# A retention and low-rank mixer kernel on one core: the first two batches handled by pairs of heads

## The chip, the core and the metric

The kernel runs on one core of one Trainium2 chip. The core has a matrix engine (TensorE, PE in the profile, with its weight loads shown apart as PEld), three elementwise engines (VectorE = DVE, ScalarE = ACT, GpSimd = POOL) and a queue engine (SyncE = SP) that here issues loads. Each engine runs its own list of instructions in order; engines wait for one another through semaphores. Matrix products are written to PSUM, a small memory of eight banks, from which DVE or ACT must copy them out. The metric is the time of one execution on the device, in microseconds (us).

## The reference

Eight batches, eight heads, 576 positions, head size 64. First a decayed causal attention without softmax, then a token mixing of rank 32 and a channel MLP with a residual:

```
scores = scale * q @ k.T ;  gamma_h = 1 - 2**(-5-h)
Dmat   = gamma_h ** (i - j)  where i >= j, else 0
x      = (scores * Dmat) @ v            # heads side by side: (B, 576, 512)
u      = x + ((x.T @ U) @ V).T          # U: 576 x 32, V: 32 x 576
out    = u + relu(u @ w_ch1) @ w_ch2    # w_ch1: 512 x 2048, w_ch2: 2048 x 512
```

Inputs and output are float32; the kernel multiplies in bfloat16.

## The kernel before

The eight batches are four couples. A couple's 1152 tokens are cut into nine chunks of 128; chunk 4 (`J`) holds the last 64 tokens of the first batch and the first 64 of the second. The decay is split into a factor on each row of `v` (`vscale`) and one on each output row (`qscale`). With that, a chunk needs four matrix steps: transposes of q and k (T), scores (SC) that DVE multiplies with a triangle of ones (mask), the product with `v` (RV), and the product of q with the running state (QS), which is itself a sum of k-transposed times v (ST). DVE then scales the result into `x` (XS). The mixer makes `a` from U and x (MA), adds V times `a` to x (MH, giving `u`) and needs `u` transposed (`uT`). Then `y1` (w1 times `uT`, 16 blocks f, line 477, Relu on ACT at line 482) and `y2` (line 511, output at line 500 and its store from POOL's queue at line 503).

From the third batch on, transposes are done by DMA, and `merge` lays attention and mixer of the next batch between the matrix products of the present one. The first two batches have their own code, and only this is touched by the change:

- `startup` (line 779) does batch 0 up to `uT`. q, k and v come in units of 256 tokens and all eight heads (`load_u`): two neighbouring tokens lie on one partition, so a DMA piece is 2 x 64 floats, 512 bytes. Batch 0 has units 0 and 1, batch 1 units 2 and 3; the 64 tokens in J are loaded apart (pieces of 256 bytes). POOL casts q and k (line 592) and scales v (line 596). T_u (607), SC_u (635), RV_u (661), QS_u (670), ST_u (687) are PE's steps of a unit. Scores and RV use halves of the array, 64 rows each. `warm(n)` (189) gives PE n products that nobody reads.
- At the end of `startup`, `x` is transposed on PE into four PSUM tiles `xT` (859), V times `a` is added there (874), and four copies (882, 884) give `uT` of batch 0.
- `first_stretch` (line 886) lays batch 1's units, its mixer (394, 421) and its transposes of `u` (`MT`, 448) between the 16 `y1` blocks of batch 0 (`y(n)` emits n of them), starts `y1` of batch 1 and returns what is left of it to `merge`.
- SP's queue carries every load of q, k, v in program order through 15 buffers `stage`. POOL's queue carries w1 (four blocks, line 195), w2 (201), and stores, between its own casts.
- PSUM: `ps_sc` (one buffer of two banks: scores), `ps_o` (one of two banks: RV and QS), `ps_s` (one bank) and `ps_big` (three).

The order of instructions on each engine is the order of the code: the schedule is written by hand.

Of the kernel before, what the change touches and what calls it, by code (L numbers as in the profile page):

```python
# [35 lines left out]
def kernel(  # L36
# [18 lines left out]
    HALF = 64  # L55
    NHP = H // 2
# [3 lines left out]
    J = 4  # L60
# [32 lines left out]
    triU = consts.tile([P, 2, P], BF16, name="triU")  # L93
    iotaU = consts.tile([P, 2, P], FP32, name="iotaU")
    posU = consts.tile([P, 4, 2, H], FP32, name="posU")
    vscaleU = consts.tile([P, 4, 2, H], FP32, name="vscaleU")
# [17 lines left out]
    def early_consts():  # L114
# [3 lines left out]
            posU, pattern=[[2 * P, 4], [1, 2], [0, H]], base=0, channel_multiplier=2,  # L118
# [3 lines left out]
            iotaU, pattern=[[-1, 2], [1, P]], base=0, channel_multiplier=-2,  # L122
# [7 lines left out]
        for h in range(H):  # L130
            nc.vector.memset(lngt[:, :, h], lng[h])
        nc.vector.tensor_scalar_add(posU[:, 2:4], posU[:, 2:4], -float(4 * P - HALF))
        nc.vector.tensor_tensor(
            out=posU.rearrange("p u j h -> p (u j) h"),
            in0=lngt[:, 0:8, :], in1=posU.rearrange("p u j h -> p (u j) h"), op=ALU.mult)
        nc.scalar.activation(out=vscaleU, in_=posU, func=AF.Exp, bias=lnb, scale=-1.0)
        nc.vector.tensor_scalar(
            out=triU[0:HALF], in0=iotaU[0:HALF], scalar1=0.0, scalar2=None, op0=ALU.is_ge)
        nc.vector.tensor_scalar(
            out=triU[HALF:P], in0=iotaU[HALF:P], scalar1=-float(P), scalar2=None,  # L140
            op0=ALU.is_ge)
# [24 lines left out]
    def make_u():  # L166
        nc.scalar.activation(out=U_E[:, 0:J, :], in_=U_f[:, 0:J, :], func=AF.Copy)
        nc.scalar.activation(out=U_E[0:HALF, J, :], in_=U_f[0:HALF, J, :], func=AF.Copy)

        ps = ps_s.tile([P, 5, R], FP32, tag="pss", name="pu_o")  # L170
        nc.tensor.matmul(ps, swap, U_E, start=True, stop=True)
        nc.scalar.activation(out=U_O[0:HALF, 1:5, :], in_=ps[0:HALF, 0:4, :], func=AF.Copy)
        nc.scalar.activation(out=U_O[HALF:P, :, :], in_=ps[HALF:P, :, :], func=AF.Copy)
# [59 lines left out]
    def cast_qk(pr, i, rows=slice(0, P), eng=None):  # L233
# [4 lines left out]
        if eng is not None:  # L238
            for j in (1, 0):
                eng.tensor_copy(  # L240
                    out=t[rows, j, :], in_=c["f", j][rows].rearrange("p h d -> p (h d)"))
            return
# [222 lines left out]
    def y1_items(par, by_seg=False):  # L465
        nch = 4 + par
        segs = [(0, 4)] if par == 0 else [(0, 3), (3, 2)]
        items = []

        def Y1(f, seg):  # L470
            if f == 0 and seg == 0:
                st["y1", par] = y1_pool.tile(
                    [P, NF, nch * P], BF16, tag=f"y1{par}", name="y1")
# [86 lines left out]
    un = [dict() for _ in range(4)]  # L560
    st["x", 0] = x_pool.tile([P, NI, dm], BF16, tag="x", name="xt")

    def unit_i0(u):
        return 2 * u + (1 if u >= 2 else 0)

    def load_u(u, which):
        b = u // 2
        t0 = 2 * P * (u % 2) + HALF * b
        for j in which:
            dram = (q, k, v)[j]  # L570
            for hh in range(2):
                t = stage.tile([P, H, D], FP32, tag="stage", name="stage_t")
                un[u]["f", j, hh] = t
                nc.sync.dma_start(  # L574
                    out=t.rearrange("p (h j) d -> p h (j d)", j=2),
                    in_=dram[b, 4 * hh:4 * hh + 4, t0:t0 + 2 * P, :].rearrange(
                        "h (p j) d -> p h (j d)", j=2),
                )

    def unit_views(u, j, hh):  # L580
        if j not in un[u]:
            un[u][j] = qk_pool.tile([P, 2, dm], BF16, tag="qk", name="qk")
        w = slice(hh * 4 * D, (hh + 1) * 4 * D)
        return (un[u][j][:, :, w].rearrange("p j (h d) -> p h j d", d=D),
                un[u]["f", j, hh].rearrange("p (h j) d -> p h j d", j=2))

    def cast_u(u, j, hh, eng):
        o, f = unit_views(u, j, hh)
        if eng is nc.scalar:
            nc.scalar.activation(out=o, in_=f, func=AF.Copy)  # L590
        else:
            eng.tensor_copy(out=o, in_=f)  # L592

    def scale_u(u, hh, eng):
        o, f = unit_views(u, 2, hh)
        eng.tensor_tensor(
            out=o, in0=f,
            in1=vscaleU[:, u, :, 4 * hh:4 * hh + 4].rearrange("p j h -> p h j")[
                :, :, :, None].to_broadcast([P, 4, 2, D]),
            op=ALU.mult,  # L600
        )

    def T_u(u, j, eng):
        pst = ps_big.tile([P, 2 * NHP, P], BF16, tag="big", name="pst")
        for jj in range(2):
            for hp in range(NHP):
                nc.tensor.transpose(
                    pst[:, jj * NHP + hp, :], un[u][j][:, jj, hp * P:(hp + 1) * P], ident)
        t = qkT_pool.tile([P, 2 * NHP, P], BF16, tag="qkT", name="qkT")
        un[u]["T", j] = t  # L610
        o, i_ = t, pst
        if j == 0:

            o = t.rearrange("p a b -> p (a b)").rearrange(
                "p (hp t j) -> p j hp t", hp=NHP, j=2)
            i_ = pst.rearrange("p (j hp) t -> p j hp t", j=2)
        if eng is nc.scalar:
            nc.scalar.activation(out=o, in_=i_, func=AF.Copy)
        else:
            eng.tensor_copy(out=o, in_=i_)  # L620

    def qT(u):
        return un[u]["T", 0].rearrange("p a b -> p (a b)").rearrange(
            "p (hp t) -> p hp t", hp=NHP)

    def SC_u(u, hh, pool_, tag):
        psc = pool_.tile([P, 2, NHP, P], FP32, tag=tag, name="psc")
        kT, qt = un[u]["T", 1], qT(u)
        for hp in range(2):
            for jj in range(2):  # L630
                for s in range(2):
                    for hl in range(2):
                        r = slice(hl * HALF, (hl + 1) * HALF)
                        m = slice(s * HALF, (s + 1) * HALF)
                        nc.tensor.matmul(  # L635
                            psc[m, hl, hp * 2 + jj, :], kT[r, jj * NHP + 2 * hh + hp, m],
                            qt[r, 2 * hh + hp, s * P:(s + 1) * P], start=True, stop=True,
                        )
        un[u]["psc", hh] = psc

    def mask_u(u, hh):
        ret = ret_pool.tile([P, H, P], BF16, tag="ret", name="ret")
        nc.vector.tensor_tensor(  # L643
            out=ret.rearrange("p (a j) i -> p a (j i)", j=2),
            in0=un[u]["psc", hh].rearrange("p a b i -> p (a b i)").rearrange(
                "p (a ji) -> p a ji", a=4),
            in1=triU.rearrange("p j i -> p (j i)")[:, None, :].to_broadcast([P, 4, 2 * P]),
            op=ALU.mult,
        )
        un[u]["ret", hh] = ret  # L650

    def RV_u(u, hh):
        if "po" not in un[u]:
            un[u]["po"] = ps_o.tile([P, 2, dm], FP32, tag="po", name="po")
        for hp in range(2):
            for hl in range(2):
                h = 4 * hh + 2 * hp + hl
                for jj in range(2):
                    for s in range(2):
                        r = slice(s * HALF, (s + 1) * HALF)  # L660
                        nc.tensor.matmul(  # L661
                            un[u]["po"][:, s, h * D:(h + 1) * D],
                            un[u]["ret", hh][r, hl * 4 + hp * 2 + jj, :],
                            un[u][2][r, jj, h * D:(h + 1) * D],
                            start=(h == 0 and jj == 0), stop=True, skip_group_check=True,
                        )

    def QS_u(u, s, slot):
        for hp in range(NHP):
            nc.tensor.matmul(  # L670
                un[u]["po"][:, s, hp * P:(hp + 1) * P],
                qT(u)[:, hp, s * P:(s + 1) * P], sblk[:, slot, hp, :],
# [3 lines left out]
    def XS_u(u, c0=0, c1=2):  # L676
        i0, n = unit_i0(u) + c0, c1 - c0
        nc.vector.tensor_tensor(  # L678
            out=st["x", 0][:, i0:i0 + n, :].rearrange("p s (h d) -> p s h d", d=D),
            in0=un[u]["po"][:, c0:c1, :].rearrange("p s (h d) -> p s h d", d=D),  # L680
            in1=qscale[:, i0:i0 + n, :, None].to_broadcast([P, n, H, D]), op=ALU.mult,
        )

    def ST_u(u, rows, acc, start):
        for hp in range(NHP):
            for jj in range(2):
                nc.tensor.matmul(  # L687
                    acc[:, hp, :], un[u][1][rows, jj, hp * P:(hp + 1) * P],
                    un[u][2][rows, jj, hp * P:(hp + 1) * P],
                    start=(start and hp == 0 and jj == 0), stop=True,  # L690
                    skip_group_check=True,
                )

    def Sblk(acc, slot):
        for hl in range(2):
            r = slice(hl * HALF, (hl + 1) * HALF)
            nc.scalar.activation(
                out=sblk[r, slot, :, hl * D:(hl + 1) * D],
# [315 lines left out]
```

## Time and profile before

| what | value |
|---|---|
| time, median of 3 runs (lowest to highest) | 335.87 us (335.54 to 336.67) |
| span of the profiled execution, first to last instruction | 335.6 us |
| instructions | 6997 |
| PE busy | 320.9 us, 96% of the span |
| PEld, DVE, ACT, POOL busy | 179.9, 138.0, 139.2, 78.2 us |
| moved by DMA | 53.17 MB, mean 158 GB/s |
| PE, first product of `y1` (line 477) starts | 32.07 us |

PE's busy time is no measure of how full it is: products overlap, and each shows a latency of about 0.2 us. The timeline gives for a row of n products the time from the first start to the last end; the start of the next row minus the start of this one, divided by n, is what one of them really takes of PE.

### The profile page before, as it was taken

To read this page: it belongs to the slowest core of one execution; us is meant where nothing else is said; L and a number is where in the kernel's file an instruction comes from. 1 tells how busy PE (TensorE), PEld (TensorE's weight loads), DVE (VectorE), ACT (ScalarE), POOL (GpSimd) and SP (SyncE) were. 2 spreads that over 40 slices of the span, in tenths; PEclk is the share of its full clock that TensorE was granted. 3 is DMA by queue.
4 is the path that set the end of the run, shared out by engine and by line. 5 is a ranking of instruction groups with operands and counts; after the bars stand their busy time and mean duration, and the time that the engine had idled before them with its cause. 6 is when DMAs were issued, how large, how long until landed. Compare 5 with 4: busy or idle time off the path is not lost.

```text
span 335.6 us, 6997 instructions
## 1 busy us (share of the span) xinstructions
PE 320.9 (96%) x2926; PEld 179.9 (54%) x2948; DVE 138.0 (41%) x190; ACT 139.2 (41%) x290; POOL 78.2 (23%) x112
## 2 busy tenths in 40 slices
PE   6688999899999999999999999999999999999996
PEld 3375554576544445446764455457754455457644
DVE  5453346433564234534356244524365144510022
ACT  2543665776210077107850176017740264037400
POOL 5686741211231140114102220222111100110000
PEclk9955999999999999999999999999999999999999
DMA  7999999999999929994998959995933400340012
GB/s 212 239 228 266 237 217 182 187 179 223 213 249 234 234 73 192 207 198 105 198 177 190 213 123 168 195 241 71 200 76 99 142 2 1 79 126 2 0 64 94
DMA packets 151311, 53.17 MB, mean 158 GB/s; under 512 B 131984, under 2 KB 148752, under 8 KB 151280
## 3 DMA queue, kind: packets, MB, share of 16 engines
q1 hardware_dynamic: 144512, 40.40, 64.7%
q0 software_dynamic: 6768, 12.32, 14.6%
q8 instruction: 23, 0.38, 0.5%
q14 instruction: 8, 0.07, 0.1%
HBM read 36.85 MB, written 9.44 MB: 138 GB/s over the span
## 4 chain that ended last, share of the span: by engine, by line
PE 91%; SPq 2%; issue 2%; DVE 2%; DMA 1%; ACT 1%; POOL 0%
PE ps_y L477 38%; PE ps_y L511 36%; PE psc L275 3%; PE po L314 2%; PE pss L687 2%; PE pss L340 2%; DMA stage_t<-in_q_dram 1%; SPq L574 1%; PE ph L421 1%; PE ps_y L522 1%; PE pa L394 1%; PE po L300 1%; PE po L661 1%; PE xT L859 1%; DVE xt L678 1%
## 5 line engine op out<-in xcount | busy, mean ns | idle before, releaser
L477 PE MATMUL ps_y<-uT,w_sb 128*128 128x256 bf16 (+2 forms) x768 | 137.0, 328 | 1.5 <-ACT uT L452 1.4
L482 ACT ACTIVATE y<-ps_y 128x384 bf16<-128x384 f32 (+2 forms) x192 | 90.0, 489 | 114.9 <-PE ps_y L477 114.2
L511 PE MATMUL ps_y<-w_sb,y 128*128 128x512 bf16 x538 | 124.3, 379 | 1.6 <-issue 0.8
L477 PEld LDWEIGHTS <-w_sb 128*128 128x128 bf16 x768 | 71.6, 98 | 46.7 <-issue 3.1
L511 PEld LDWEIGHTS <-y 128*128 128x128 bf16 x560 | 52.4, 98 | 60.3
L500 DVE TENSOR_TENSOR o_sb<-ps_y,u 128x512 f32<-128x512 f32 (+2 forms) x38 | 25.2, 663 | 76.6 <-PE ps_y L511 74.4
L503 POOL DMA_DIRECT2D out_dram<-o_sb x31 | 17.3, 558 | 158.6 <-DVE o_sb L500 152.8
L285 DVE TENSOR_TENSOR ret<-psc,tri 128x1024 bf16<-128x1024 f32 x24 | 29.4, 1225 | 47.3 <-PE psc L275 47.3
L254 POOL TENSOR_TENSOR vt<-stage_t,vscale 128x512 bf16<-128x512 f32 (+1 forms) x29 | 30.0, 1047 | 50.6 <-DMA stage_t<-in_v_dram 50.1
L325 DVE TENSOR_TENSOR xt<-po,qscale 128x512 bf16<-128x512 f32 x27 | 18.6, 691 | 25.9 <-PE po L314 25.9
L427 DVE TENSOR_TENSOR u<-ph,xt 128x768 bf16<-128x768 f32 (+2 forms) x24 | 21.8, 951 | 13.5 <-PE ph L421 13.5
L348 ACT ACTIVATE s_sb<-pss 128x512 bf16<-128x512 f32 x24 | 14.3, 597 | 8.3 <-PE pss L340 7.3
L245 ACT ACTIVATE qk<-stage_t 128x512 bf16<-128x512 f32 x27 | 16.5, 622 | 2.1 <-DVE o_sb L500 2.1
L243 DVE CAST qk<-stage_t 128x512 bf16<-128x512 f32 x27 | 16.3, 604 | 0.0
L400 ACT ACTIVATE a_sb<-pa 128x128 bf16<-128x128 f32 x8 | 2.2, 276 | 33.0 <-PE pa L394 33.0
L643 DVE TENSOR_TENSOR ret<-psc,triU 128x1024 bf16<-128x1024 f32 x8 | 9.7, 1222 | 11.3 <-PE psc L635 11.3
L314 PEld LDWEIGHTS <-ret 128*128 128x128 bf16 x216 | 10.0, 98 | 4.2
L592 POOL CAST qk<-stage_t 128x512 bf16<-128x512 f32 x16 | 9.6, 611 | 7.0 <-DMA stage_t<-in_q_dram 5.3
L275 PEld LDWEIGHTS <-qkT 64*128 64x128 bf16 x216 | 6.1, 94 | 9.1 <-issue 8.7
L275 PE MATMUL psc<-qkT 64*128 64x128 bf16 x216 | 10.7, 219 | 0.0
L314 PE MATMUL po<-vt,ret 128*128 128x64 bf16 x216 | 10.7, 193 | 0.0
L340 PE MATMUL pss<-vt,qk 128*128 128x128 bf16 (+1 forms) x96 | 9.3, 219 | 0.0
(103 smaller groups left out, 165.5 us busy)
## 6 DMA issues: line engine op xcount, KB each, us to landing
stage_t<-in_k_dram SPq DMA_DIRECT2D x32, 256.0 KB, 4.1
stage_t<-in_q_dram SPq DMA_DIRECT2D x32, 256.0 KB, 4.9
stage_t<-in_v_dram SPq DMA_DIRECT2D x32, 256.0 KB, 5.5
out_dram<-o_sb POOLq DMA_DIRECT2D x31, 256.0 KB, 3.8
w_sb<-in_moe_w_ch_dram POOLq DMA_DIRECT2D x4, 512.0 KB, 8.4
w_sb<-in_moe_w_ch_dram POOLq DMA_DIRECT2D x8, 256.0 KB, 10.2
stage_t<-in_k_dram SPq DMA_DIRECT2D x8, 128.0 KB, 4.2
stage_t<-in_q_dram SPq DMA_DIRECT2D x8, 128.0 KB, 4.0
```

What stands on the lines that cost most here:

```text
L245: nc.scalar.activation(out=t[rows, 0, :], in_=c["f", 0][rows].rearrange("p h d -> p (h d)"), func=AF.Copy)
L254: (eng or nc.gpsimd).tensor_tensor(out=c["v"][rows], in0=c["f", 2][rows], in1=vscale[rows, i, :, None].to_broadcast([n, H, D]), op=ALU.mult,)
L275: nc.tensor.matmul(psc[:, hl, hp, :], qkT[r, NHP + hp, :], qkT[r, hp, :], start=True, stop=True,)
L285: nc.vector.tensor_tensor(out=ret.rearrange("p (hp hl) i -> p hl hp i", hl=2), in0=c["psc"], in1=m[:, None, None, :].to_broadcast([P, 2, N ...
L314: nc.tensor.matmul(c["po"][:, hl, hp * D:(hp + 1) * D], c["ret"][:, h, :], c["v"][:, h, :], start=(first and hp == 0), stop=True, skip_gro ...
L325: nc.vector.tensor_tensor(out=xt[:, i, :].rearrange("p (hp hl d) -> p hl hp d", hl=2, d=D), in0=c["po"][:, :, 0:NHP * D].rearrange("p hl ( ...
L427: nc.vector.tensor_tensor(out=st["u", par][:, i0 - base:i0 - base + n, w].rearrange("p s (c d) -> p c s d", c=2), in0=ph[k][:, :, 0:n, :], ...
L477: nc.tensor.matmul(ps[:, 0:n, :], w1_sb[:, cc, f * P:(f + 1) * P], st["uT", par][:, c0:c0 + n, cc, :], start=(cc == 0), stop=(cc == NCC - 1),)
L482: nc.scalar.activation(out=st["y1", par][:, f, c0 * P:(c0 + n) * P], in_=ps[:, 0:n, :].rearrange("p s t -> p (s t)"), func=AF.Relu)
L500: nc.vector.tensor_tensor(out=o_sb[:, 0:n], in0=ps[:, 0:n], in1=st["u", par][:, c, w], op=ALU.add)
L503: (nc.sync if last else nc.gpsimd).dma_start(out=out_flat[r0:r0 + P, w], in_=o_sb[:, 0:n])
L511: nc.tensor.matmul(ps, st["y1", par][:, f, c * P:(c + 1) * P], w2_sb[:, f, :], start=(f == 0), stop=(f == NF - 1),)
```

## The change

Units of 256 tokens with all heads become pairs of heads (two heads, 512 tokens, four neighbouring tokens on one partition). A batch is four pairs and the 64 tokens of J, which now lie on partitions 0 to 63 for both batches. Each pair has its own tiles from the load to `uT`. Products whose rows were halves of a unit (64) are now quarters (32). `uT` of batch 1 is made from transposed `x` as in batch 0; the transposes of `u` (`MT`) are gone. Twelve `warm` products remain of 21. w1 is issued after the casts of batch 0's last pair. `make_u` is split: U_E in `startup`, U_O in `first_stretch`. Two prefetches of the next couple and their preparation move behind batch 1's chain. The mask of a unit is replaced by one for four tokens (`tri4`, `vscale4`).

```diff
-    def load_u(u, which):
+    def load_h(b, hp, which):
+        t0 = HALF * b
+        for j in which:
+            t = stage.tile([P, H, D], FP32, tag="stage", name="stage_t")
+            sl[b][hp]["f", j] = t
+            nc.sync.dma_start(
+                out=t.rearrange("p (h j) d -> p h (j d)", j=4),
+                in_=(q, k, v)[j][b, 2 * hp:2 * hp + 2, t0:t0 + 4 * P, :].rearrange(
+                    "h (p j) d -> p h (j d)", j=4),
+            )
...
+    def T_h(b, hp, ek, eq):
+        c = sl[b][hp]
+        pst = ps_big.tile([P, 2 * NHP, P], BF16, tag="big", name="pst")
+        for n, j in ((0, 1), (1, 0)):
+            for jj in range(4):
+                nc.tensor.transpose(pst[:, 4 * n + jj, :], c["qk"][:, j, jj, :], ident)
+        t = qkT_pool.tile([P, 2 * NHP, P], BF16, tag="qkT", name="qkT")
...
+        copy(ek, c["kT"], pst[:, 0:4, :])
+        copy(eq, c["qT"].rearrange("p (t j) -> p j t", j=4), pst[:, 4:8, :])
+
+    def SC_h(b, hp):
...
+        for j in range(4):
+            for s in range(4):
+                for hl in range(2):
+                    r = slice(hl * HALF, (hl + 1) * HALF)
+                    m = slice(s * Q, (s + 1) * Q)
+                    nc.tensor.matmul(
+                        psc[m, hl, j, :], c["kT"][r, j, m], c["qT"][r, s * P:(s + 1) * P],
+                        start=True, stop=True,
+                    )
...
+    def ST_h(b, hp, engs):
+        acc = ps_s.tile([P, 4, D], FP32, tag="pss", name="acc")
...
+        for n in range(4):
+            rows = (n + 1 if b == 0 else n) * Q
+            for j in range(4 if rows else 0):
+                for hl in range(2):
+                    add(hl, n, c["qk"][0:rows, 1, j, hl * D:(hl + 1) * D],
+                        c["v"][0:rows, j, hl, :])
+        for hl, eng in enumerate(engs):
+            r = slice(hl * HALF, (hl + 1) * HALF)
+            copy(eng, sblk[r, :, hp, hl * D:(hl + 1) * D], acc[r])
+
+    def RQ_h(b, hp, a, spare=False):
...
+        for hl in range(2):
+            for j in range(4):
+                for e in range(2):
+                    s = 2 * a + e
+                    m = slice(s * Q, (s + 1) * Q)
+                    nc.tensor.matmul(
+                        po[:, e, hl * D:(hl + 1) * D],
+                        c["ret"][m, hl * 4 + j, :], c["v"][m, j, hl, :],
+                        start=(hl == 0 and j == 0), stop=True, skip_group_check=True,
+                    )
+        for e in ((1, 0) if b == 1 or a == 1 else (1,)):
...
+    def MA_h(b, hp, eng):
+        g = slice(hp * R, (hp + 1) * R)
+        pa = ps_s.tile([P, P], FP32, tag="pss", name="pa")
+        for n in range(5):
...
+        copy(eng, st["a", b][g, :], pa[g, :])
+
+    def XT_h(b, hp):
...
+    def UT_h(b, hp, engs):
...
+    def UT_J(c0, eng):
...
     def startup():
+        load_h(0, 0, (1, 0, 2))
+        load_h(0, 1, (1, 0, 2))
+        load_J(0)
+        load_v_rows()
+        load_u_rows()
+        load_h(0, 2, (1, 0, 2))
+        load_h(0, 3, (1, 0, 2))
+        load_J(1)
+        for hp in range(NHP):
+            load_h(1, hp, (1, 0, 2))
...
+        warm(10)
+        pool_h(0)
+        T_h(0, 0, nc.vector, nc.scalar)
+        warm(2)
+        SC_h(0, 0)
...
+        T_h(0, 2, nc.vector, nc.scalar)
+        RX(1, 1)
+        J_h(0)
+        J_h(1)
+        XT_h(0, 0)
+        make_ue()
+        SC_h(0, 2)
+        mask_h(0, 2)
+        pool_h(3, True)
+        load_w1(0)
+        MA_h(0, 0, nc.scalar)
+        MA_h(0, 1, nc.scalar)
+        ST_h(0, 2, AD)
+        T_h(0, 3, nc.vector, nc.scalar)
+        RX(2, 0)
+        UT_h(0, 0, (nc.scalar,))
+        XT_h(0, 1)
+        RX(2, 1)
+        SC_h(0, 3)
+        mask_h(0, 3)
+        scale_h(0, 3, nc.gpsimd, slice(0, 1))
+        scale_h(0, 3, nc.vector, slice(1, 2))
+        load_w1(1)
+        load_w1(2)
+        load_w1(3)
+        J_h(2)
+        UT_h(0, 1, (nc.scalar,))
+        XT_h(0, 2)
+        MA_h(0, 2, nc.scalar)
+        ST_h(0, 3, (nc.scalar, nc.vector))
+        UT_h(0, 2, (nc.scalar,))
+        RX(3, 0)
+        RX(3, 1, True)
+        J_h(3)
+        XT_h(0, 3)
+        MA_h(0, 3, nc.scalar)
+        UT_h(0, 3, (nc.scalar, nc.vector))
 
     def first_stretch():
+        cast_J(1, nc.gpsimd)
+        scale_J(1, nc.gpsimd)
+        y(2)
+        make_uo()
+        T_J(1)
+        y(1)
+        SC_J(1)
...
+        for hp in range(NHP):
+            cast_h(1, hp, 1, nc.gpsimd)
+            cast_h(1, hp, 0, nc.gpsimd)
+            scale_h(1, hp, nc.gpsimd)
+            T_h(1, hp, nc.vector, nc.scalar)
+            if hp:
+                XT_h(1, hp - 1)
+                MA_h(1, hp - 1, nc.vector)
             y(1)
+            SC_h(1, hp)
+            mask_h(1, hp)
+            ST_h(1, hp, (nc.scalar, nc.scalar))
             y(1)
+            if hp:
+                UT_h(1, hp - 1, (nc.vector,))
+            RQ_h(1, hp, 0)
+            XS_h(1, hp, 0)
             y(1)
+            RQ_h(1, hp, 1)
+            XS_h(1, hp, 1)
         for f in range(0, NF, 2):
             load_w2(f)
+        XT_h(1, 3)
+        MA_h(1, 3, nc.scalar)
+        UT_J(0, nc.scalar)
         y(16)
+        UT_h(1, 3, (nc.scalar, nc.vector))
+        UT_J(2, nc.scalar)
...
```

`RQ_h` is RV and then QS for half a of the pair's tokens. `XT_h` is four transposes of `x` into one tile of `ps_big`, `UT_h` adds V times `a` on top (one product of 512 columns) and copies to `uT`; `UT_J` does the same for chunk J, two column blocks at a time. `RX(hp, a)` is `RQ_h(0, hp, a)` followed by its XS; `J_h(hp)` is RV, QS and XS of pair hp for the 64 tokens of J; `pool_h(hp)` is POOL's two casts and the scaling of v.

| products on PE for batch 1 | before | after |
|---|---|---|
| scores (SC) | 64 | 128 |
| RV | 64 | 128 |
| ST | 24, and 4 for J | 104 |
| transposes of `u`, or of `x` for `uT` | 20 | 20, and 12 that add V times `a` |
| T, QS, MA, MH, J's T, SC and RV | 32, 16, 20, 24, 24 | the same |

## The prediction

> **What bounds the kernel now.** I read first the busy shares by slice, with the granted clock under them.
>
> ```profile
> PE   6688999899999999999999999999999999999996
> PEclk9955999999999999999999999999999999999999
> ```
>
> One slice is 8.4 us. PE is full from the third slice to the end; a full PE at clock 5 is half as fast. Next, the stages around the change, by windows (start:end, length, then busy us of PE, PEld, DVE, ACT, POOL with counts, granted clock, DMA share, GB/s):
>
> ```profile
> 15.00:20.00 5.00, 3.84 (x65) 2.78 (x65) 4.58 (x4) 2.72 (x7) 4.91 (x5) 0.78 1.24 188
> 20.00:25.00 5.00, 5.00 (x91) 4.09 (x89) 1.23 (x1) 2.17 (x7) 3.76 (x7) 0.50 1.18 273
> 25.00:30.00 5.00, 4.64 (x62) 3.80 (x57) 1.81 (x2) 1.14 (x5) 1.89 (x4) 0.50 1.19 260
> 30.00:35.00 5.00, 4.33 (x31) 1.72 (x29) 1.93 (x3) 2.41 (x5) 4.89 (x7) 0.51 1.19 257
> 35.00:40.00 5.00, 5.00 (x53) 2.66 (x52) 0.85 (x3) 4.03 (x7) 2.80 (x4) 1.00 1.26 252
> ```
>
> By single microseconds the clock falls at 17.9 us and comes back at 34.9. From 20 us on no other engine is full; in `first_stretch` DVE and ACT stay under 70%. Third, what PE waited for between 31.5 and 66 us, batch 1's stretch (total us, times, longest):
>
> ```profile
> PE ps_y L477 <- ACT uT L452: 1.4, 1, 1.4
> PE pst L708 <- ACT uT L882: 0.7, 1, 0.7
> PE ph L421 <- DVE u L427: 0.6, 1, 0.6
> ```
>
> That is 2.7 us in 34. So from 31.6 us on PE's own work sets the end, and whatever is added to it there comes out at the end. Before 31.6 it is batch 0's chain. Last, PE's timeline (start, length, what) for prices:
>
> ```profile
> 39.42 0.42 PE L635 MATMUL psc<-qkT 64*64 64x128 bf16 x16
> 39.77 1.04 PE L477 MATMUL ps_y<-uT,w_sb 128*128 128x512 bf16 x4
> 40.74 0.62 PE L687 MATMUL pss<-qk 64*128 64x128 bf16 x8
> 41.29 0.42 PE L635 MATMUL psc<-qkT 64*64 64x128 bf16 x16
> ...
> 44.81 0.41 PE L661 MATMUL po<-qk,ret 64*128 64x64 bf16 x16
> 45.15 1.07 PE L607 MATMUL pst<-ident,qk 128*128 128x128 bf16 x16
> ...
> 54.81 0.71 PE L394 MATMUL pa<-xt,U_O 128*32 128x128 bf16 x20
> 55.46 1.04 PE L477 MATMUL ps_y<-uT,w_sb 128*128 128x512 bf16 x4
> ```
>
> From start to next start: a score product takes 0.35/16 = 22 ns, RV 0.34/16 = 21, ST 0.55/8 = 69, MA 0.65/20 = 33, a transpose 56 (the 16 at 45.15 are followed at 46.05), a y1 block 0.97 us. At half clock: RV 32 ns (30 in 0.96 us in the chain), ST 121 (16 at 22.16, next row at 24.09), a transpose 116 (12 in 1.39).
>
> **Batch 1's stretch, part by part** (counts from the change's table, prices from those rows).
>
> - SC: 64 more products. Scores use a 64 by 64 corner of the array and stream 128 columns, RV 64 rows, all columns and 64 streamed, yet both cost 21 to 22 ns: that looks like a price per instruction, and a 32-row product does half the work for it. 64 x 22 = +1.4 us.
> - RV: 64 x 21 = +1.4.
> - ST: 104 products of 64 columns for 24 + 4. Consecutive ones use the same rows and alternate column halves. Lower bound 22 ns each, upper 46 (J's RV, eight at 52.16 followed at 52.53, all in one corner of the array); nearest is MA (same rows, other columns), 33. Old: 24 x 69 + 4 x 82 (35.51 to 35.84) = 2.0. So 3.4 - 2.0 = +1.4, bounds +0.3 and +2.8.
> - `uT`: 20 transposes of `u` go (-1.2: 0.65 + 0.54 in the timeline). In come 16 transposes of `x` (+0.9), four products of 512 columns (0.97/4 each, +1.0) and J's 12 (+0.7). Net +1.4.
> - MA: 20 both times, but five in a row now write the same 32 columns: 56 ns like a transpose, not 33: +0.45. U_O's product: +0.1.
>
> Sum +6.2, bounds +5.1 and +7.6. Waits: the 2.7 us go with `MT`; the new end of the chain has no y1 left to cover it (16 blocks are used up in the loop): XS 0.42 (DVE's 1024 elements take 1.22, 512 take 0.69, so 256 take 0.42) plus 0.15 to pass on, the ACT copy of `a` 0.3, the copies to `uT` 0.4 to 0.8, with the small products between: 1.8; three waits of 0.2 for XS at the pair boundaries. Together 2.4, so -0.3. The stretch gets **+5.9 us**. POOL, DVE and ACT cover: a pair has POOL 2 x 0.61 + 1.05 = 2.3, DVE 0.4 + 0.3 + 1.22 + 0.6 + 2 x 0.42 = 3.4, ACT 0.7 + 2 x 0.38 + 3 x 0.6 = 3.3 us, in a period on PE of three y1 (2.9) plus 3.9. w1's later blocks have 8.4 us median to landing and some 6 us a block of four f. The prefetches moved behind the chain keep their place in SP's queue; their casts come about 7 us before `merge` needs them.
>
> The Trainium skill weighs against the cut: *TensorEngine Tiling (Array Packing)*, section Performance Considerations, says that each matmul has about 60 cycles of overhead and warns against taking the tiling factor from a dimension that is already small (RV has 64 columns). At 2.4 GHz, 60 cycles would be 25 ns, and SC plus RV +3.2 in place of +2.8; the rows say 21 to 22.
>
> **Startup.** *Loads.* Tiles of 256 KB in 512-byte pieces came about 1.0 us apart (first cast at 3.77, J's q cast at 13.94: ten tiles plus V and U). J's 128 KB in 256-byte pieces took as long, so pieces count, not only bytes. Pieces of 1024 bytes: bounds 0.5 us a tile (by pieces) and 1.0 (by bytes); packets of 256 bytes cost 25 ns of an engine at 84 to 100 us and those of 512 about 31, so I take 0.8. The last q of batch 0 (11 tiles of 0.8, three of J at 1.05, V and U 0.9, first at 3.7) then lands near 15.8, with 12.8 and 17.8 as bounds. POOL casts 0.6 later: hp3 is ready at 16.4.
>
> *PE's chain.* PE is not there yet: it meets T, SC, ST, RV in order, each waiting for a copy of the one before, and `ps_o` and `ps_s` have one buffer each. At full clock, with 0.15 per hand-over, T of pair 2 starts at 13.6 (behind ACT's copies of J and V, which run to 14.4). Then: T, RX(1,1) and both J_h to 15.9; SC 16.6; MA, copy, MA, copy through the one bank 18.0; ST 18.8; T(3) 19.2; ACT's two state copies and the qT copy let RX(2,0) end at 19.9, RX(2,1) 20.8; SC(3) 21.5; mask 1.22 to 22.8; DVE's half of scale (0.6) 23.4; J's XS 23.7; MA(2) and copy 24.4; ST(3) 25.2; copies and RX(3,0) 25.8, RX(3,1) 26.2, XS 26.7, J_h XS 27.0; MA, copy 27.8; UT 28.1; copies 28.6. The first y1 would start at **28.7**, 2.9 us before the old stretch began (31.56). Earlier loads shift little of it.
>
> *Clock.* In the old startup PE lost its full clock at 17.9 with 21 `warm` products in place and no wait over 1.8 us, and dense work of small products from 18.3 to 31 did not bring it back; only y1 did. The new startup has 12 warm products, the last at about 6 us, and more gaps. I expect half clock by about 18. PE pieces on the chain from there sum to 5.8 us at full clock; times 1.45 (32/22, price per instruction) to 2 (columns) this adds 2.6 to 5.8; I take 3.5, so y1 starts at **32.2**, +0.6 against 31.56. The old stretch also began at half clock, so the loss there cancels.
>
> Against the row stands *TensorE: Matmul & The Clock Gate* (Part 1 and its closing table): the clock falls only after an idle window of about 3.4 us, and gaps under some 3 us are safe. By that rule y1 starts at 28.7 and the sum is 339; the row, where it fell without such a gap, decides.
>
> **Sum.** 335.6 + 5.9 + 0.6 = 342.1; the runs' median stands 0.3 above the profiled span. I state **342 us**.
>
> **Rivals.**
> 1. *The clock holds through startup.* For: in 4.3 to 17.9 a mix about as thin kept it. Against: the fall at 17.9. Then -2.9 + 5.9, and no half clock in the first y1 blocks (31.5 to 34.9 cost 1.7): +1.3, 337; with ST at its lower bound 336.
> 2. *Faster: startup is shorter than my chain.* Mechanism: loads at 0.5 us a tile, and hand-overs that hide under other pairs, so that y1 starts as soon as w1 is there. Place: the first block of w1, issued behind hp3's casts (14 at the earliest) and 7.3 to 8.4 us in flight (23); then -8.6 + 5.1 and -1.7 for the half clock that is not met: 330; with y1 at 26 and the stretch at +5.9, 334. It decides from a start of y1 before about 27.4 with a full clock, or 25.7 with half. Against: the single banks and mask-to-XS chains above.
> 3. *Half clock bites more.* Lost by 11 us, all of PE's chain doubles: y1 at 35 to 36, or the clock falls again between single y1 blocks of the pair loop (43% of its time is y1, about 50% before): 346 to 349.
>
> **How the numbers follow.** Forecast (339 to 345) 0.48, rival 1 0.17, rival 2 0.18, rival 3 0.17. A measurement of this kernel tells 0.3%, 1 us, from no change: up to 334.8 is faster, from 336.9 slower. Faster: rival 2, 0.18; same: the low part of rival 1 and the top of rival 2's reach, 0.07; slower 0.75. The range leaves out the lower half of rival 2 and the top of rival 3: 334 to 347.
>
> **What would show it.** In the changed profile: first y1 at 32 (28.7 or less means rivals 1 or 2); granted clock 0.5 around 20 to 32; SC and RV rows at 21 to 22 ns a product (if 11, the stretch shrinks by 2.8); ST between 22 and 46; from the first y1 to the same point of y1 of batch 1 (in the old trace 31.56 to about 65.3), 5.9 us more. PE waits in that stretch above 3 us, for POOL or w1, would make it wrong, as would a second fall of the clock.

## The result, and the profile after

| | before | after |
|---|---|---|
| time, median of 4 runs each (lowest to highest) | 335.71 us (334.29 to 336.67) | 353.98 us (353.75 to 356.38) |
| ratio, with its 95% interval | | 1.056 (1.052 to 1.061) |
| span of the profiled execution | 335.6 us | 352.0 us |
| PE's stretch on batch 1 starts | 31.56 us | 38.82 us |
| first product of line 275 (scores of the third batch, in `merge`) starts | 67.78 us | 87.35 us |

The change is slower by 18 us; the forecast was 342, its range ended at 347. The rest of this section finds the 16.4 us between the two spans. From the first product of line 275 to the end the kernel before takes 335.6 - 67.78 = 267.8 us and the changed one 264.65; in the changed kernel three more blocks f of batch 1's `y1` stand ahead of that product (3.2 us), so behind it nothing differs. All 16.4 us arise ahead of it: 38.82 - 31.56 = **7.3 us in startup**, and (87.35 - 38.82 - 3.2) - (67.78 - 31.56) = **9.1 us in batch 1's stretch**. The prediction had 0.6 and 5.9.

The busy shares by slice of the kernel after, one slice 8.8 us, with the granted clock under them:

```profile
PE   7888989989999999999999999999999999999996
PEclk9555599999999999999999999999999999999999
```

Four slices at half clock where the kernel before had two. The windows (start:end, length, busy us of PE, PEld, DVE, ACT, POOL with counts, clock, DMA share, GB/s):

```profile
5.00:10.00 5.00, 3.78 (x74) 2.42 (x74) 2.10 (x3) 1.31 (x1) 2.71 (x5) 1.00 1.17 254
10.00:15.00 5.00, 3.36 (x105) 2.75 (x105) 2.15 (x4) 3.36 (x6) 2.84 (x4) 0.53 1.04 280
15.00:20.00 5.00, 4.91 (x78) 3.18 (x75) 2.12 (x5) 2.88 (x7) 4.90 (x8) 0.50 1.09 225
...
40.00:45.00 5.00, 5.00 (x28) 1.89 (x27) 0.00 (x0) 2.45 (x6) 4.62 (x7) 0.55 0.85 185
```

The microsecond from 10 to 11 us has a mean clock of 0.67, so the clock falls at about 10.3 us (the expectation of a_warm has 10.7), not at about 18, and is back at about 44.5. From 15 us on PE is busy 78 to 100% of each window: it is a slow PE, not a waiting one, that fills startup. What came before the fall stands in PE's timeline (start, length, what; in brackets the wait before it and its cause):

```profile
5.61 1.06 PE L610 MATMUL pst<-ident,qk 128*128 128x128 bf16 x8
6.46 0.83 PE L190 MATMUL pw<-ident 128*128 128x512 bf16 x2
8.52 0.42 PE L624 MATMUL psc<-qkT 64*32 64x128 bf16 x32 [1.22 <-ACT qkT L581]
```

and the next scores, at 11.98, waited 1.64 us for the copy of their pair; that wait began as the clock fell. *TensorE: Matmul & The Clock Gate*, Part 1, in the Trainium skill says that the clock falls after an idle window of about 3.4 us; here the longest wait of PE between its first product and the fall was 1.22 us, and the kernel before lost its clock with none above 1.8, so the measurement decides.

Why the copy is late shows in the groups of ACT between 5 and 47 us (output <- input, count | busy us, mean ns of one | idle before, and what ended it):

```profile
L581 ACT ACTIVATE qkT<-pst 128x512 bf16<-128x512 bf16 x4 | 5.2, 1304 | 6.5 <-DVE qkT L583 6.5
L734 ACT ACTIVATE qkT<-pst 128x512 bf16<-128x512 bf16 x2 | 1.2, 597 | 0.0
```

Two things that the prediction did not have. ACT's copy of q-transposed waits for DVE's copy of k-transposed (0.42 us, at the second pair behind a mask of 1.23): both read one PSUM tile `pst`, and the program orders the two readers, as a_split below shows. The 6.5 us are ACT's; of PE's time two waits for this copy took 2.9 in startup. And the copy takes 1304 ns, while the same 512 elements written without a step (J's, line 734) take 597; the copy of a pair writes every fourth element. I had taken 0.7.

Now the stretch, at full clock, in PE's timeline of the kernel after:

```profile
48.98 0.42 PE L624 MATMUL psc<-qkT 64*32 64x128 bf16 x32 [1.23 <-ACT qkT L581]
49.33 1.02 PE L646 MATMUL acc<-vt,qk 64*64 64x256 bf16 x26
50.28 1.04 PE L478 MATMUL ps_y<-uT,w_sb 128*128 128x512 bf16 x4
51.25 0.41 PE L678 MATMUL po<-vt,ret 32*128 32x64 bf16 x16
51.59 0.28 PE L685 MATMUL po<-sblk,qkT 128*128 128x128 bf16 x2
...
53.58 0.52 PE L803 MATMUL xT<-ident,xt 128*128 128x128 bf16 x4
54.03 0.45 PE L792 MATMUL pa<-xt,U_O 128*32 128x128 bf16 x5
54.41 1.04 PE L478 MATMUL ps_y<-uT,w_sb 128*128 128x512 bf16 x4
```

From start to next start: 32 scores in 0.35 us, 11 ns each (I had 22); RV 16 in 0.34, 21 each (as taken); ST 26 in 0.95 (37 each; I had 33); MA five in 0.38, 76 (I had 56). So PE's extra work is: SC 0; RV +1.4; ST 4 x 0.95 - 2.0 = +1.8; `uT` (transposes of x 1.8, V times `a` 0.85 and J's part 1.0 against 1.2 of `MT`) +2.45; MA 4 x 0.38 - 0.65 = +0.9; U_O +0.2. That is 6.75. The first part, at half clock until 44.5, loses an estimated 2.5 against 1.4 before (its rows at both clocks): +1.1; the waits (1.23 above and some seven of 0.2 to 0.4) come to about 0.3 more than before's 2.7. Sum 8.15 of 9.1; about 1 us is not accounted for.

### The profile page after: what moved, and what is told of

It reads as the page before. It is cut to its first block, busy times and chain, and to the rows that moved or that the text cites. A ratio compares the mean times of both kernels' runs of the same rounds, so it can differ in the third digit from the quotient of the medians.

```text
span 352.0 us, 7884 instructions
## 1 busy us (share of the span) xinstructions
PE 337.7 (96%) x3348; PEld 188.7 (54%) x3371; DVE 142.9 (41%) x219; ACT 144.0 (41%) x299; POOL 77.5 (22%) x111
## 4 chain that ended last, share of the span: by engine, by line
PE 92%; ACT 4%; DVE 2%; issue 1%; POOL 0%; POOLq 0%; DVEq 0%
PE ps_y L478 36%; PE ps_y L512 35%; PE psc L275 3%; ACT qkT L581 2%; PE acc L646 2%; PE po L314 2%; PE po L678 2%; PE pss L340 2%; PE pw L190 1%; PE ph L421 1%; PE psc L624 1%; PE po L685 1%; PE ps_y L523 1%; PE pst L610 1%; PE po L300 1%
## 5 line engine op out<-in xcount | busy, mean ns | idle before, releaser
L478 PE MATMUL ps_y<-uT,w_sb 128*128 128x256 bf16 (+2 forms) x768 | 138.5, 330 | 0.1
L504 POOL DMA_DIRECT2D out_dram<-o_sb x31 | 17.3, 559 | 163.6 <-DVE o_sb L501 157.8
L285 DVE TENSOR_TENSOR ret<-psc,tri 128x1024 bf16<-128x1024 f32 x24 | 29.4, 1224 | 45.6 <-PE psc L275 45.6
L254 POOL TENSOR_TENSOR vt<-stage_t,vscale 128x512 bf16<-128x512 f32 x27 | 28.0, 1051 | 59.4 <-DMA stage_t<-in_v_dram 49.5
L325 DVE TENSOR_TENSOR xt<-po,qscale 128x512 bf16<-128x512 f32 x27 | 18.6, 690 | 24.2 <-PE po L314 23.6
L427 DVE TENSOR_TENSOR u<-ph,xt 128x1024 bf16<-128x1024 f32 (+2 forms) x24 | 21.8, 951 | 14.0 <-PE ph L421 14.0
L245 ACT ACTIVATE qk<-stage_t 128x512 bf16<-128x512 f32 x27 | 16.4, 621 | 3.2 <-DMA stage_t<-in_q_dram 3.2
L581 ACT ACTIVATE qkT<-pst 128x512 bf16<-128x512 bf16 x8 | 10.4, 1306 | 10.1 <-DVE qkT L583 10.1
L633 DVE TENSOR_TENSOR ret<-psc,tri 128x1024 bf16<-128x1024 f32 x8 | 9.8, 1224 | 10.8 <-PE psc L624 10.8
L583 POOL CAST qk<-stage_t 128x512 bf16<-128x512 f32 (+1 forms) x18 | 10.9, 616 | 7.4 <-DMA stage_t<-in_q_dram 4.7
L275 PE MATMUL psc<-qkT 64*128 64x128 bf16 x216 | 10.7, 219 | 0.0
L314 PE MATMUL po<-vt,ret 128*128 128x64 bf16 x216 | 10.7, 193 | 0.0
```

Source lines behind the costliest of these rows:

```text
L254: (eng or nc.gpsimd).tensor_tensor(out=c["v"][rows], in0=c["f", 2][rows], in1=vscale[rows, i, :, None].to_broadcast([n, H, D]), op=ALU.mult,)
L275: nc.tensor.matmul(psc[:, hl, hp, :], qkT[r, NHP + hp, :], qkT[r, hp, :], start=True, stop=True,)
L285: nc.vector.tensor_tensor(out=ret.rearrange("p (hp hl) i -> p hl hp i", hl=2), in0=c["psc"], in1=m[:, None, None, :].to_broadcast([P, 2, N ...
L314: nc.tensor.matmul(c["po"][:, hl, hp * D:(hp + 1) * D], c["ret"][:, h, :], c["v"][:, h, :], start=(first and hp == 0), stop=True, skip_gro ...
L325: nc.vector.tensor_tensor(out=xt[:, i, :].rearrange("p (hp hl d) -> p hl hp d", hl=2, d=D), in0=c["po"][:, :, 0:NHP * D].rearrange("p hl ( ...
L427: nc.vector.tensor_tensor(out=st["u", par][:, i0 - base:i0 - base + n, w].rearrange("p s (c d) -> p c s d", c=2), in0=ph[k][:, :, 0:n, :], ...
```

## The experiments

"Startup" is the start of the stretch on batch 1 (in forms like the changed kernel, the first `y1`), "merge" the first product of line 275. Each row is one profiled execution; the four times of the changed kernel lay 2.6 us apart, so differences of a microsecond between rows tell nothing unless the trace shows their place.

| run | startup us | merge us | span us | clock |
|---|---|---|---|---|
| before | 31.56 | 67.78 | 335.6 | 0.974 |
| after | 38.82 | 87.35 | 352.0 | 0.951 |
| a_warm | 36.42 | 84.40 | 349.0 | 0.995 |
| a_split | 37.29 | 83.98 | 348.6 | 0.956 |
| a_lean | 33.01 | 82.55 | 347.2 | 0.99 |
| a_split_lean | 32.19 | 78.90 | 343.5 | 0.995 |
| u0p1 | 25.41 | 71.83 | 336.4 | 1.0 |
| p0u1b | 37.8 | 75.3 | 343.1 | 0.955 |

In the rows that run batch 1 by pairs, span less merge is 264.6 each time: what is won ahead of merge arrives whole at the end.

**The clock, and the shared PSUM tile.** Three runs: 62 unread products of 512 columns in the places where PE waits; k and q transposed into two PSUM tiles; and the swap of one batch's form, told below.

```diff
# a_warm
         T_h(0, 0, nc.vector, nc.scalar)
-        warm(2)
+        warmb(8)
         SC_h(0, 0)
...
+        warmb(8)
         SC_h(0, 1)
# a_split
-        pst = ps_big.tile([P, 2 * NHP, P], BF16, tag="big", name="pst")
-        for n, j in ((0, 1), (1, 0)):
+        pk = ps_big.tile([P, NHP, P], BF16, tag="big", name="pk")
+        pq = ps_big.tile([P, NHP, P], BF16, tag="big", name="pq")
+        for ps, j in ((pk, 1), (pq, 0)):
             for jj in range(4):
-                nc.tensor.transpose(pst[:, 4 * n + jj, :], c["qk"][:, j, jj, :], ident)
+                nc.tensor.transpose(ps[:, jj, :], c["qk"][:, j, jj, :], ident)
...
```

> The changed kernel with 62 unread 512-column products put into PE's waits of the startup (from 6 us to the last UT), to hold the clock. Theory A (the half clock from 10.7 to 44 us is the larger part of the loss in startup): clock 1.0 through most of 10 to 38 us, first y1 at 30 to 33 us in place of 38.8, span 344 to 347. Theory B (the chain of copies between engines sets startup whatever the clock): clock restored but first y1 at 36 or later, span 350 to 353.

> The changed kernel with k's and q's transposes of a pair in two PSUM tiles, so that ACT's copy of qT need not come after DVE's copy of kT. Theory B (chain of copies): first y1 3 to 4 us earlier (four times 0.42, and 1.2 where DVE's copy stood behind a mask), and the 1.2 us wait of the stretch's first pair gone: span 347 to 349. Theory A (half clock, PE's own pieces): first y1 at most 1.5 us earlier, span 350 to 351.5.

a_warm held the clock at 1.0 through startup, yet `y1` began only 2.4 us earlier: 62 products are some 13 us of PE, more than the waits had room for. Neither theory's ranges were met (`y1` at 36.4, span 349.0). a_split took 3.4 us off the span: 1.5 in startup, where PE's waits fell from 5.5 to 3.9 us, which is the bound of theory A, and 1.8 in the stretch, so that the span is theory B's. Its ACT group reads

```profile
L581 ACT ACTIVATE qkT<-pq 128x512 bf16<-128x512 bf16 x5 | 6.5, 1309 | 4.6 <-PE pq L611 4.6
```

ACT waits for PE's transposes now and for DVE no more; the copy is as long as before, so its length comes from the step of its output and not from sharing the tile. Both copies still write one tile `qkT` in SBUF, so it was the PSUM tile that ordered them. Since a_warm was overfilled, a leaner filling (25 of these products, at the same kind of places), alone and with the split:

> The changed kernel with 25 unread products in the startup in place of 2 (a_warm had 62 that took 13 us of PE and stood in the way). Theory A (PE's small pieces at half clock set startup): the clock holds and first y1 comes at 30 to 33 us, span 343 to 346. Theory B (copies between engines): the clock holds and first y1 stays above 35, span 347.5 or more. If the clock falls, it tells nothing.

> As a_lean, and k's and q's transposes in two PSUM tiles. At half clock the split was worth 3.4 us of span. If both theories hold and add: first y1 1.5 to 3 us before that of a_lean, and the stretch 1 us shorter; span 340 to 343.

The windows of a_lean:

```profile
15.00:25.00 10.00, 9.42 (x200) 5.93 (x201) 4.63 (x10) 5.60 (x13) 9.82 (x14) 1.00 1.15 227
25.00:31.00 6.00, 5.27 (x119) 3.12 (x118) 3.41 (x6) 2.11 (x5) 1.69 (x3) 1.00 1.18 246
...
40.00:45.00 5.00, 3.76 (x82) 2.15 (x82) 1.23 (x2) 3.06 (x5) 4.74 (x8) 0.81 0.96 197
45.00:50.00 5.00, 4.85 (x77) 2.40 (x75) 1.55 (x4) 2.44 (x3) 4.24 (x6) 0.85 1.09 175
```

With the clock held startup ends at 33.0, 5.8 us earlier, the edge of theory A, and the span of 347.2 is above its range. These 5.8 us, or more, as the unread products stand partly in the way, are what the half clock costs the changed kernel; they are no part of the 7.3 us between the two kernels, as the kernel before was at half clock too (the next table). But the clock falls later, in the loop over pairs of batch 1 (0.81 and 0.85 in these windows), so the span gained only 4.8. In the run with the split the loop loses less, both in waiting and in clock: 343.5, 8.5 us of the 16.4 recovered. `y1` starts 0.8 us before that of a_lean (1.5 to 3 expected), and the span is just above its range; whether the split kept the clock in the loop, one run can't tell. PE's longest waits there from 25 to 90 us are

```profile
PE psc L631 <- ACT qkT L587: 0.5, 1, 0.5
PE xT L810 <- DVE xt L700: 0.4, 1, 0.4
```

so what is left of the loss, 7.9 us, is hardly waiting. A part is the clock again, in the thin end of batch 1's chain:

```profile
65.00:70.00 5.00, 4.64 (x27) 2.66 (x27) 1.09 (x3) 2.97 (x8) 0.00 (x0) 0.72 0.14 28
```

0.72 over 5 us is 2.8 us at half clock, which costs 1.4 us at most; the rest is work of PE, the unread products included.

**One batch at a time.** u0p1 has batch 0 by units as before and batch 1 by pairs; p0u1 and p0u1b the reverse.

```diff
# u0p1, in startup
-        load_h(0, 0, (1, 0, 2))
...
+        load_u(0, (1, 0, 2))
# p0u1, in first_stretch
-        for hp in range(NHP):
-            cast_h(1, hp, 1, nc.gpsimd)
...
+        unit(2, (0, 1, 2), False)
+        unit(3, (2, 3), True)
```

> Batch 0 by units as in the kernel before, batch 1 by pairs as in the changed one. If the two halves of the loss add (startup 7.3, stretch 9.2): first y1 at about 32, span 343 to 345. If the stretch was long only because it began late and cold: 337 to 340.

> Batch 0 by pairs as in the changed kernel, batch 1 by units as in the kernel before. If the halves add: first y1 at about 39, span 342 to 345. If batch 1's form matters little: 349 to 352.

> The change's batch 0 by pairs with before's batch 1 by units, with the constants of the unit form made only after the first pairs (in p0u1 they stood ahead of everything and PE waited 4.1 us for the first copy). Theory (the loss is the sum of two independent parts, startup +7 and batch 1's stretch +8 to +9): y1 starts at 38 to 39.5, from there to the first L275 product as long as before, span 342 to 344. Rival (the parts share one cause, as a late arrival of what merge needs, which absorbs part of a later y1): span 337 to 340.

p0u1 (348.5, span 346.6, between its two ranges) made the constants of both forms at the start, and PE waited 4.1 us for its first copy: a fault of the experiment, so p0u1b makes them later (one run, 345.1 us, span 343.1, as its theory had it). The granted clock by slices, first of u0p1, then of p0u1b:

```profile
PEclk9999999999999999999999999999999999999999
```

```profile
PEclk9755599999999999999999999999999999999999
```

p0u1b is 7.5 us above before: its startup ends 6.2 us later, and its stretch (75.3 - 37.8 = 37.5 us) is 1.3 longer than before's 36.2, as the clock comes back only at 43 us, 4.4 after the first `y1` in place of 2.8. So batch 0 by pairs costs its own 7.5 us. u0p1 kept a full clock, which startup by units does in some executions; its stretch takes 71.83 - 25.41 - 3.2 = 43.2 us, against 36.2 - 1.4 = 34.8 for before at full clock: +8.4, with no part in it for the clock. Its time (one run, 338.6 us) hardly shows that, as startup ended 6.2 us earlier; both of its forecasts had `y1` and the span later than that. The two losses are separate, and 7.5 + 8.4 = 15.9 is nearly the whole 16.4; that it comes so near is partly luck, as each figure rests on one execution and the 7.5 holds the 1.3 us of clock in the stretch.

What startup is made of can be summed from PE's timeline, from the first transposes to the start of the stretch: the rows of the kernel's own products (from start to next start, without the idle time between), the unread products, and PE's waits.

| us | own rows | unread | waits | sum |
|---|---|---|---|---|
| before (half clock from 17.8) | 17.2 | 3.0 | 6.4 | 26.7 |
| after (half clock from 10.3) | 26.9 | 0.8 | 5.5 | 33.2 |
| u0p1 (units, full clock) | 12.5 | 2.9 | 4.4 | 19.8 |
| a_lean (pairs, full clock) | 17.5 | 7.2 | 2.7 | 27.4 |

So the 7.3 us are PE's own rows, +9.6, less 2.2 of unread products and 0.9 of waits, and the first transposes start 0.7 later. The waits did not grow. At full clock pairs have 5.0 us more of PE's own work in batch 0 than units, and the half clock makes the difference 9.6.

**What one product of ST costs.** a_split_lean without 72 of the 104 ST products of batch 1.

```diff
-            for j in range(4 if rows else 0):
+            for j in range(0 if not rows else 4 if b == 0 else 1):
```

> a_split_lean with 9 of the 12 state products of each head left out in batch 1 (three of the four tokens of each partition are missing from batch 1's running state, so the output is not the reference's). Per pair 18 products fewer, 72 in all. Theory (PE's own products in the pair loop lie bare on the path and cost what the timeline says, 37 ns each): 4 x 0.66 = 2.7 us less; the first L275 product at 76.2 in place of 78.9, span 340.8 in place of 343.5. Rival 1 (their time is hidden, the loop waits for masks and copies anyway, as ST stands between SC and RV and covers DVE's mask): PE waits for DVE's mask or ACT's copies instead, gain under 1 us. Rival 2 (the start of merge is set by transfers as in the kernel before): first product earlier, but the span not below 342.5.

The span stayed (343.4), as startup, whose code is the same, ended 1.1 us later (33.3 against 32.19): here the granted clock fell in it after all, to a mean of 0.66 from 25 to 30 us, in spite of the 25 unread products. The rows decide. a_split_lean, then a_st1:

```profile
53.17 1.02 PE L653 MATMUL acc<-vt,qk 64*64 64x256 bf16 x26
54.13 1.04 PE L484 MATMUL ps_y<-uT,w_sb 128*128 128x512 bf16 x4
```

```profile
53.69 0.74 PE L653 MATMUL acc<-vt,qk 64*64 64x256 bf16 x8
54.36 1.04 PE L484 MATMUL ps_y<-uT,w_sb 128*128 128x512 bf16 x4
```

26 products take 0.96 us and 8 take 0.67: the 18 cost 0.29 us, 16 ns each and not 37, and 4 x 0.29 = 1.2 us is what the stretch lost (from the first `y1` to merge, 45.5 against 46.7). My theory of 2.7 us falls; the place was right (no new wait, so nothing hides ST), the price per product was not. Most of ST's 0.95 us stays with eight products: two for J of 256 columns and six in three row counts (32, 64, 96). Whether the change of row count or J's products set it was not tried.

**Would an earlier `y1` have paid?** The kernel before with more unread products keeps its clock and starts `y1` earlier. b_warm adds 21, b_warm2 ten.

```diff
# b_warm2
-        warm(2)
+        warm(8)
         T_J(LO)
...
         mask_J(LO)
+        warm(4)
```

> The kernel before, with 21 more unread products behind the startup's waits from 13 us on. u0p1 by chance kept its clock and began y1 at 25.4. If the half clock from 17.9 to 34.9 cost the kernel before as much: clock 1.0, first y1 at 26 to 28, span 329 to 332. If its startup is bound by copies and loads: 334 to 337.

> As b_warm with 10 more products only, all before 18.5 us. If it is enough to bridge the waits at 13.0 to 14.6 and 17.3 to 18.3: as b_warm or 1 us faster, 328 to 331. If the small products behind them cannot hold the clock: falls at about 21 or 25, 332 to 336.

b_warm: 335.3 us, ratio 1.001 (0.997 to 1.006); b_warm2: 336.5, 1.001 (0.998 to 1.005). Both missed their forecasts of a gain. b_warm starts `y1` at 29.43 and merge at 65.29, 2.5 us ahead of before, with no wait for a transfer; its profiled execution kept that (span 333.4), but its nine times spread from 334.9 to 339.0 at mean clocks of 0.995 or more, and what spreads them was not traced. b_warm2 starts `y1` at 27.57, 4.5 us earlier than before, and gains nothing. Its waits of PE, and SP's queue (start, length of the issue):

```profile
PE psc L275 <- DMA qkT<-qk: 1.4, 1, 1.4
PE ps_y L477 <- ACT y L482: 1.4, 1, 1.4
```

```profile
53.95 4.42 SPq L228 DMA_DIRECT2D stage_t<-in_q_dram  x1
58.46 2.44 SPq L228 DMA_DIRECT2D stage_t<-in_v_dram  x1
61.08 1.89 SPq L262 DMA_TRANSPOSE qkT<-qk  x1
```

PE now waits for the third batch: the transpose of chunk 9 stands in SP's queue behind the loads of chunk 11. So the last two kernels put the preparation ahead of those loads; b_fast_late also moves chunk 10's preparation behind the first `y1` of batch 1.

```diff
# b_fast = b_warm2 and
-        for fn in aux[:2]:
-            fn()
+        aux[1]()
+        aux[0]()
...
-        for fn in aux[2:]:
-            fn()
+        aux[3]()
+        aux[2]()
```

> The kernel before with ten more unread products in startup (as b_warm2) and, in first_stretch, the preparation of chunks 9 and 10 put ahead of the loads of chunks 11 and 12, so that SP's queue issues the DMA transpose of chunk 9 before the loads of chunk 11 (in b_warm2 it stood behind them until 61.08 us). Theory A (an earlier y1 was worth nothing to the kernel before because SP's order held back chunk 9's transpose): merge's first L275 product starts at 61 to 63 in place of 65.4, PE waits for the DMA transpose of qkT less than 0.5 us there, span 331 to 334, about 0.99 of before. Theory B (the DMA queues are full, whatever the order): L275 again at 65 or later, span 335 to 337, the same as before. If the later loads now come late, the wait moves to the next chunk and the span is 335 to 338.

> b_fast, with the preparation of chunk 10 moved behind the first y1 products of batch 1, so that ACT's cast of chunk 10 (it waited 2.6 us for its load in b_warm2) does not hold back Relu. Theory A: PE's wait for ACT's Relu copies (1.4 us in b_warm2) goes, span 0.5 to 1.5 below b_fast, 330 to 333. Theory B: the same as before, 335 to 337. Rival: chunk 10's own transpose is now late and PE waits for it at the second group of scores, 1 to 2 us, span not below b_fast.

b_fast: 335.6 us, 0.999 (0.994 to 1.004); b_fast_late: 337.4, 1.003 (0.998 to 1.007). In b_fast the transpose is issued at 50.05 and merge begins at 61.8, 6.0 us ahead of before, as theory A had it, but without theory A's gain. At 112.7, where batch 2's `y1` begins, PE waits for the DMA transpose of its `u`:

```profile
PE ps_y L477 <- DMA uT<-u: 2.0, 1, 2.0
```

```profile
L438 SPq DMA_TRANSPOSE uT<-u x1: 3849/3849/3849, 105.8 to 105.8; - x1
```

In before that transpose is issued at 107.0, and its `y1` of batch 2 begins at 116.6 without a wait: PE was still 5.9 us ahead, the transfer 1.2. Behind the wait of 2.0 the granted clock falls to 0.50 for some 3.4 us (113.9 to 117.4), by my estimate another 1.7. That is nearly all of the 3.8 us by which b_fast takes longer than before from merge to the end (271.6 against 267.8). In b_fast_late, which was to be faster than b_fast, the wait for chunk 9 was back (1.1), Relu was held up 2.4, and batch 2's `u` came 2.5 late. Of the 6.0 us that b_fast earned, the transfer and the clock behind it took back 3.8; the 2.2 left in that one execution don't show in the medians. No version here beats the kernel before by what can be measured.

## Why the prediction was wrong, point by point

**What bounds the kernel: right for work that is added.** PE's own work from `y1` on set the end: what runs with pairs won ahead of merge they kept whole, and the two forms' losses stood apart. Of time that the kernel before wins ahead of merge it is not true: b_warm2 and b_fast lost most of it again behind late transfers.

**Direction right, size wrong: 354 against 342, outside the range.** Of the 9.9 us that the sum lacked, 6.7 are startup (7.3 for 0.6) and 3.2 the stretch (9.1 for 5.9). In startup pair 2's transposes start 4.3 us late (17.9 for 13.6), and from there to the first `y1` it takes 20.9 us for the forecast's 15.1 at full clock plus 3.5, another 2.3. Three steps failed.

- *"I expect half clock by about 18."* It fell at 10.3. The step carried the old time of the fall over to a startup with 9 `warm` products fewer and a new wait at 7.3 us. So PE's rows from the second scores (11.98) to pair 2's transposes took 5.8 us where the same rows at full clock take 3.6 (a_lean): 2.2 of the 4.3. Rival 3 named the mechanism ("Half clock bites more", `y1` at 35 to 36); it still took the fall at 11 as its worst case and stopped 3 us short, and it had 0.17.
- *"PE pieces on the chain from there sum to 5.8 us at full clock."* This term was too small. From the second scores to the first `y1` PE's own rows take 15.1 us at full clock (a_lean), 11.6 of them from pair 2's transposes on, and they lay on the path almost whole: 24.2 us in the changed kernel, with 2.7 of waits. From pair 2's transposes on the half clock added 6.8 us to them (18.4 for 11.6) where the forecast had 3.5; a part of that replaced waits. The chain at full clock was near for this part: a_lean takes 16.1, with 3.3 of unread products in it.
- *"with 0.15 per hand-over"*, and 0.7 for ACT's qT copy. The copy took 1304 ns and stood behind DVE's. Both were readable before the run: line 618's copy with a step of two took 1.31 for 1024 elements where the plain one took 1.02, and the code gives one PSUM tile to two engines, which the old transposes never did. The other 2.1 of the 4.3 us I put down to PE's two waits for this copy, 1.2 and 1.6 us; that is argued and not isolated. The shared tile alone was worth 1.5 us of startup at half clock (a_split) and 0.8 at full clock (a_split_lean); what the longer copy cost by itself was not tried.

**The stretch: +9.1 for +5.9.** Mis-sized terms: SC +1.4 was 0; ST +1.4 was +1.8; `uT` +1.4 was +2.45; MA +0.45 was +0.9; waits -0.3 were +0.3; "the loss there cancels" (half clock at the start) was +1.1. RV +1.4 was right, and so was the period of a pair, 2.9 plus 3.9, by luck in part, as the error of SC and those of ST, `uT` and MA offset each other: from the transposes of one pair to those of the next it is 6.83. SC's "price per instruction" is refuted by the row itself, 11 ns for a product on half the columns, though RV, on half the rows, stayed at 21. *TensorE: Matmul & The Clock Gate*, Part 3, says that products on different parts of the array overlap, each adding about 4 ns; 11 and 16 ns here are above that, but nearer to it than to 22 and 37. The overhead of 60 cycles that the prediction cited from *TensorEngine Tiling (Array Packing)* would be 25 ns by the estimate given there; the rows of SC and ST lie below it. ST's total came near although its price per product was wrong, as a_st1 shows.

**Loads, w1 and DMA: right that they don't limit startup.** PE waited for no load in startup; hp3's cast of q ended near 17.3 (forecast 16.4). "The prefetches moved behind the chain" cost nothing visible; the DMA queues of the changed kernel stood nearly empty from 65 to 75 us, while merge came so late that nothing missed them.

**Rivals 1 and 2.** The clock did not hold. When it was held through startup (a_lean), the span was 347, not 337: startup ended at 33.0 and not at 28.7, with 7.2 us of unread products in it, the stretch is longer by its own work, and the clock fell in it. Rival 2, a shorter startup, did not come about; whether time won there would have met late transfers, as in b_fast, no run of the changed kernel shows, as none reached merge that early.

## What to carry to other kernels

Price a copy by how its output is strided and by who else reads the same PSUM tile: two readers are one after the other, and one tile per reader costs only a buffer. In a phase of many small products sum PE's own rows before taking it for a chain of waits, and treat the clock as part of the schedule: count the unread products that an edit removes, and the gaps it opens. Before working for an earlier start, follow the queue of transfers to the next stage: if that stage starts when its data comes, the time won ahead of it is lost in front of it, and a wait there can cost the clock besides.

## What the runs showed of the hardware

- The clock of the changed kernel fell when PE had waited no longer than 1.22 us at a time, and from 15 to 39 us PE, busy 78 to 100% with small products, did not restore it; 25 products of 512 columns strewn over the waits held it in a_lean and a_split_lean, not all through in a_st1 (0.66 from 25 to 30 us).
- ACT took 1304 ns for 512 elements a row written at every fourth place, 597 for the same written in a row.
- Small products on separate parts of the array cost 11 ns (64 rows by 32 columns) and 16 ns (ST), but a row of eight ST products still took 0.67 us.
- Startup by units kept its clock in u0p1 and lost it in the profile of before, with the same 21 `warm` products; startup ended at 25.4 there and at 31.6 here. The kernel's time follows by little: in two series of runs of before the median of those with a mean clock under 0.988 was 337.1 and 337.5 us, that of the others 335.8 both times.
